# A decode kernel's units in another order behind the second change of layer, and one result row from its own memory

## The chip, the cores and the metric

The kernel runs on one NeuronCore of a Trainium2 chip. The metric is the device time of one execution in microseconds, taken as the median of several runs. The core has TensorE (PE in the profile; PEld is its weight load), VectorE (DVE), ScalarE (ACT), GpSimd (POOL) and SyncE (SP). Here SP issues nearly all DMAs, in program order, and 16 DMA engines carry them out.

## The reference

Two layers, each an attention with a KV cache and then a token mixer, on one new token of B = 2 batches with D = 512 channels:

```
x = x + A(layernorm(x));  x = x + Mix(layernorm(x))      # twice, with the same weights and caches
A:   q = x @ wq (32 heads of 128);  8 kv heads, 4 query heads on each
     p = softmax(q . k_cache / sqrt(128)) over 32768 keys;  o = p @ v_cache;  o @ wo
Mix: u = gelu(layernorm(x)^T * w1 + b1)   (512 x 1792);  u @ w2 + b2
```

Each kv head of each batch has 16 MiB of K and 16 MiB of V in float32, and both layers read all of them: 1 GiB in all. The weights wq and wo of one head together are 2 MiB.

## The kernel before

**Units.** The work is cut into 32 units (layer, batch, head), written out as the list `units` (lines 186 to 191). A unit is 8 chunks of K and 8 of V, each 2 MiB (128 partitions by CK = 4096 columns). Step s belongs to chunk s % 8 of unit s // 8, so there are 256 steps, and a tail.

**One step** (the loop at lines 706 to 722), in this order: issue the load of K chunk s (`load_k`, line 256), multiply it with the query (`k_chunk`, the matmuls of line 277), run the work listed under `pre` for that step, issue the load of V chunk s − 10 (`load_v`, line 332: a unit's V follows its K ten steps later), multiply it with the exponentials in S (`v_chunk`, line 390), run the work listed under `post`. The order on every engine is this program order; nothing is rearranged. Below, K170 is the K chunk of step 170 and V170 the V chunk taken up in step 170, chunk 0 of unit 20. In steps 0 to 93 and from 176 on, two steps go together, with loads of 4 MiB.

**Where the loads go.** One big tile `mem` holds cells of 4096 columns. `buffer` (line 112) hands out the cell, or pair of cells, used least recently: six cells in the paired steps, three (RING) in steps 97 to 175. A load into a cell waits on SP until PE has used what lay there before. In steps 170 to 178 that means: K171 takes the cell of K169, K172 that of V169, V172 that of K170, K173 that of K171, K174 that of K172, K175 that of V172, V175 that of K173. K176, a pair, takes cells in which kept V chunks lie that are read in steps 173 and 174. V178 takes those of K174 and V175.

**Kept V.** Behind the three ring cells lies `kept`: 51 of the 64 parts of V of head 7 (the keeper) that layer 0 loads for one batch and layer 1 reads again (`KEPT`, line 25; `stays`, line 328). Unit 20, (1, 1, 7), reads it in steps 170 to 177: chunks 0, 1, 3, 4, 6 and 7 wholly kept, chunk 2 in part, chunk 5 loaded. Unit 15, (1, 0, 7), does the same for batch 0 in steps 130 to 137. Outside the unpaired steps the ring borrows the cells of kept chunks 1, 3 and 4.

**Weights.** Heads 4 to 7 (RESIDENT) have homes of their own for their weights and load them once. Heads 0 to 3 (`passing`) share the cells of kept chunks 0, 6, 7 and again 0, and are loaded twice: once in layer 0 and, as the kept V has lain there in between, again for unit (1, 0, h). `load_weights` (line 97) is issued in `post` of step s0 − 6 of that unit, where s0 is the unit's first step (lines 661 to 663). `make_q` (line 228) computes the unit's query from wq in steps s0 − 4 and s0 − 3, so between other units' chunks; `out_1` and `out_2` (lines 423, 438) add the unit's result through wo to the batch's row at step s0 + 18.

**Mixer.** When a batch's last unit of a layer is done, `mix_1`, `mix_2`, `hidden_tile`, `hidden_out` and `mix_4` run in the following steps; for (layer 1, batch 0), whose last unit is number 28, `mix_4` (line 628) stands at step 251. It takes S[1] (`row_tile`, line 197), one of the two tiles of exponentials, as memory for the result row, and ACT issues the DMA to `out` from there. The next transpose of scores into S[1] (`turn_scores`, line 308) is that of unit 30 in the same step. Batch 1 ends with unit 31 in `last_mixer`.

Of the kernel before, what the change touches and what calls it, by code (L numbers as in the profile page):

```python
# [36 lines left out]
def gqa_mixer_kernel(ctx: ExitStack, tc: tile.TileContext, x, kt, v, wqo, cols, out):  # L37
# [16 lines left out]
    nc = tc.nc  # L54
    B, D = out.shape
# [30 lines left out]
    kept_columns = sum(KEPT.values()) * QT * DH  # L86
    heads = list(range(HKV))
    passing = [h for h in heads if h not in RESIDENT]
# [3 lines left out]
    kept = mem[:, KEPT0 : KEPT0 + kept_columns]  # L92
# [30 lines left out]
    b2c = cols_sb[:, 3 * FT : 3 * FT + 1]  # L123
# [59 lines left out]
    ends = [h for h in RESIDENT[1:]]  # L183
    keeper = HKV - 1
    assert RESIDENT[0] == keeper and len(ends) == BRIDGE and LAYERS == 2 and B == 2
    units = [(0, b, h) for h in passing for b in range(B)]
    units += [(0, 0, h) for h in ends + [keeper]]
    units += [(0, 1, h) for h in ends] + [(1, 0, keeper), (0, 1, keeper)] + [(1, 0, h) for h in ends]
    units += [(1, 1, keeper), (1, 1, ends[0])]
    units += [(1, b, h) for h in passing for b in range(B)]  # L190
    units += [(1, 1, h) for h in ends[1:]]
    assert sorted(units) == sorted((a, b, h) for a in range(LAYERS) for b in range(B) for h in heads)
    lay = {(a, b): [u for u in units if u[:2] == (a, b)] for a in range(LAYERS) for b in range(B)}

# [2 lines left out]
    def row_tile():  # L197

        return S[HALVES - 1]
# [17 lines left out]
    def unit_of(n):  # L217

        return units[n]
# [230 lines left out]
    ysb, px = {}, {}  # L450
# [177 lines left out]
    def mix_4(key):  # L628

        layer, b = key  # L630
        p = px[key]
        nc.tensor.matmul(p, sel1, ysb[key], start=False, stop=True, skip_group_check=True)
        ysb[key] = row_tile()
        if layer == LAYERS - 1:
            nc.vector.tensor_scalar_add(ysb[key], p, b2c)
            nc.scalar.dma_start(out[b : b + 1, :], ysb[key][:1, :])
        else:
            nc.vector.tensor_copy(ysb[key], p)
            st = work.tile([P, 6], F32, name="ln_st")
            mv = work.tile([P, 2], F32, name="ln_mv")  # L640
            rs = work.tile([P, 1], F32, name="ln_rs")
            nc.vector.bn_stats(st, p)
            nc.vector.bn_aggr(mv, st)
            nc.vector.tensor_scalar_add(rs, mv[:, 1:2], EPS)
            nc.gpsimd.tensor_tensor(rs, rs, half_neg, op=ALU.pow)
            stats[key] = mv, rs
# [7 lines left out]
    for n in range(NU):  # L654
        layer, b, h = unit_of(n)
# [23 lines left out]
        if units[n] == lay[layer, b][-1]:  # L679
            key = (layer, b)  # L680
            at(pre, e - 1, mix_1, key)
            at(post, e, take_rows, key)
            at(pre, e + 1, mix_2, key)
            for f in range(FT + 1):
                k, v_side = divmod(f + 1, 2)

                if f:
                    at(post if v_side else pre, e + 1 + k, hidden_out, key, f - 1, rank=0)
                if f < FT:
                    at(post if v_side else pre, e + 1 + k, hidden_tile, key, f, rank=2)  # L690
            at(post, e + 8, take_rows, key)
            at(pre, e + 9, mix_4, key)
            if layer + 1 < LAYERS:
                at(pre, e + 9, to_columns, key)
# [76 lines left out]
```

## Time and profile before

| what | value |
|---|---|
| median of 3 runs | 2538.9 us (2536.26 to 2538.92) |
| the profiled execution's own time | 2542.73 us |
| its span, first to last instruction | 2541.0 us |
| mean granted TensorE clock | 0.797 |
| busy: PE, PEld, DVE, ACT, POOL | 64%, 17%, 8%, 8%, 0% |
| read from HBM | 1072.20 MB, 422 GB/s over the span |

The profile is of one execution. Busy shares say how long an engine had an instruction running; the DMA share of a stretch is the mean over the 16 DMA engines. A bracket behind an instruction gives how long its engine stood idle before it and what released it; "<-DMA mem<-in_kt_dram" is a K load. Rows of SPq in a timeline are the moments at which SP issued a DMA; an "x3" merges three issues in a row. A row of a timeline with x16 is one 2 MiB chunk on PE, with x32 a pair.

### The profile page before, as it was taken

The page shows a single profiled execution, that of the slowest core. Times are in us where ns is not written, and L with a number is a line of the kernel's source. Part 1 is how long each engine was busy: PE and PEld are TensorE (multiplying, and loading weights), DVE is VectorE, ACT ScalarE, POOL GpSimd, SP SyncE. Part 2 cuts the span into 40 slices and gives each one's busy share as a digit, 9 for nine tenths or more (in the row PEclk, how much of TensorE's full clock was granted, in tenths as well). Part 3 has the DMA queues.
Part 4 walks back from the last instruction along what each step waited for, and adds up shares of the span by engine and source line. Part 5 has one row for each costly group of instructions (what it writes and reads, how often), then busy time and mean ns, then how long its engine had stood idle before and what let it go on. Part 6 is the DMA issues. An engine that isn't in the chain of part 4 may idle for free.

```text
span 2541.0 us, 21411 instructions
## 1 busy us (share of the span) xinstructions
PE 1619.8 (64%) x9700; PEld 426.5 (17%) x9700; DVE 193.5 (8%) x494; ACT 194.6 (8%) x577; POOL 4.9 (0%) x17
## 2 busy tenths in 40 slices
PE   5565656666565666776576765666665666666666
PEld 1111111111111111211121111111111111111112
DVE  1000000000000000110000110010000000000102
ACT  0000000000000000120000110010000000000112
POOL 0000000000000000000000000000000000000000
PEclk8777787777777788888888898787778777778877
DMA  9999999999999999999999999899999999999996
GB/s 413 435 430 429 432 431 431 431 430 433 431 431 430 431 427 428 416 428 421 427 416 426 428 427 427 338 426 429 432 433 430 431 431 430 432 431 430 430 425 283
DMA packets 50068, 1073.58 MB, mean 423 GB/s; under 512 B 5813, under 2 KB 5817, under 8 KB 6458
## 3 DMA queue, kind: packets, MB, share of 16 engines
q1 hardware_dynamic: 49688, 1072.19, 98.7%
q8 instruction: 76, 1.25, 0.2%
q14 instruction: 14, 0.11, 0.0%
q10 hardware_dynamic: 290, 0.03, 0.0%
HBM read 1072.20 MB, written 0.00 MB: 422 GB/s over the span
## 4 chain that ended last, share of the span: by engine, by line
DMA 76%; PE 22%; DVE 1%; issue 0%; ACT 0%; SPq 0%
DMA mem<-in_v_dram 40%; DMA mem<-in_kt_dram 36%; PE scores L277 10%; PE acc L390 10%; PE misc L235 2%; PE misc L247 0%; PE rows L609 0%; DVE hid L244 0%; PE misc L428 0%; PE rows L573 0%; PE misc L419 0%; ACT S L314 0%; ACT hid L620 0%; ACT mem L583 0%; ACT mem L594 0%
## 5 line engine op out<-in xcount | busy, mean ns | idle before, releaser
L390 PE MATMUL acc<-mem,S 128*16 128x512 f32 x4092 | 692.7, 824 | 426.0 <-DMA mem<-in_v_dram 421.1
L277 PE MATMUL scores<-mem,qpad 128*32 128x512 f32 x4096 | 638.1, 767 | 404.0 <-DMA mem<-in_kt_dram 393.3
L314 ACT ACTIVATE S<-S,neg 128x128 f32<-128x128 f32 x256 | 130.5, 513 | 2140.9 <-DVE neg L305 1735.3
L390 PEld LDWEIGHTS acc<-mem,S 128*16 128x16 f32 x4092 | 137.3, 120 | 914.9 <-issue 537.9
L277 PEld LDWEIGHTS scores<-mem,qpad 128*32 128x32 f32 x4096 | 152.7, 132 | 817.3 <-issue 604.3
L235 PE MATMUL misc<-mem,xnT 128*1 128x512 f32 x256 | 118.9, 602 | 1.6 <-issue 1.6
L287 DVE TENSOR_REDUCE mx<-scores 128x1 f32<-128x512 f32 x64 | 44.2, 691 | 464.6 <-PE scores L277 451.1
L428 PE MATMUL misc<-selg,S 128*128 128x4 f32 x248 | 35.3, 266 | 31.1 <-DVE S L425 31.1
L609 PE MATMUL rows<-hid,cols_sb 128*1 128x512 f32 x84 | 49.0, 668 | 8.6 <-ACT hid L620 8.6
L421 DVE RECIPROCAL rl<-misc 128x4 f32<-128x4 f32 x32 | 5.8, 183 | 617.0 <-PE misc L419 617.0
L247 PE MATMUL misc<-one,hid 1*128 1x1 f32 x256 | 33.5, 248 | 29.8 <-DVE hid L244 29.8
L309 DVE STREAM_TRANSPOSE S<-scores 128x512 f32<-128x512 f32 x64 | 44.8, 701 | 90.0 <-PE acc L390 84.3
L314 ACT ACTIVATION_READ_ACCUMULATOR S<-S,neg 128x1 f32 x256 | 47.8, 187 | 0.0
L297 DVE TENSOR_REDUCE m<-misc 1x4 f32<-1x128 f32 x32 | 8.9, 279 | 504.4 <-PE misc L295 504.4
L428 PEld LDWEIGHTS misc<-selg,S 128*128 128x128 f32 x248 | 33.2, 208 | 61.0 <-issue 60.0
L620 ACT ACTIVATE hid<-bcast,bias,scale 128x512 f32<-128x512 f32 x42 | 32.7, 778 | 127.5 <-PE rows L609 111.2
L247 PEld LDWEIGHTS misc<-one,hid 1*128 1x128 f32 x256 | 30.8, 186 | 59.5 <-DVE hid L244 59.5
L441 PE MATMUL rows<-mem,oT 128*1 128x512 f32 x248 | 37.8, 637 | 0.0
L235 PEld LDWEIGHTS misc<-mem,xnT 128*1 128x1 f32 x256 | 19.1, 84 | 70.5 <-issue 69.8
L425 DVE COPY S<-acc 128x512 f32<-128x512 f32 x31 | 21.2, 684 | 84.8 <-PE acc L390 84.8
L244 DVE COPY hid<-misc 1x512 f32<-1x512 f32 x32 | 21.4, 668 | 74.6 <-PE misc L235 71.4
L305 DVE TENSOR_SCALAR neg<-misc 128x4 f32<-128x4 f32 x32 | 5.2, 161 | 245.5 <-PE misc L303 245.5
(109 smaller groups left out, 201.7 us busy)
## 6 DMA issues: line engine op xcount, KB each, us to landing
mem<-in_kt_dram SPq DMA_DIRECT2D x87, 4096.0 KB, 23.7
mem<-in_v_dram SPq DMA_DIRECT2D x85, 4096.0 KB, 24.0
mem<-in_kt_dram SPq DMA_DIRECT2D x82, 2048.0 KB, 12.7
mem<-in_v_dram SPq DMA_DIRECT2D x69, 2048.0 KB, 12.6
mem<-in_wqo_dram SPq DMA_DIRECT2D x12, 2048.0 KB, 28.1
mem<-in_v_dram SPq DMA_DIRECT2D x4, 1280.0 KB, 20.9
mem<-in_v_dram SPq DMA_DIRECT2D x2, 768.0 KB, 22.9
mem<-in_v_dram SPq DMA_DIRECT2D x1, 1024.0 KB, 23.5
```

The source lines that it names most:

```text
L235: nc.tensor.matmul(q_ps[n][:1, :], xnT[layer, b][:, d : d + 1], wq_sb[h][:, d, :], start=(d == 0), stop=(d == DT - 1),)
L244: nc.vector.tensor_copy(q_row[n][:1, :], q_ps[n][:1, :])
L247: nc.tensor.matmul(pt[:, r : r + 1], q_row[n][:1, r * DH : (r + 1) * DH], one[:1, :], start=True, stop=True)
L277: nc.tensor.matmul(sc_ps[n, half][32 * g : 32 * g + 32, :], q, kc[:, (k * NG + g) * w : (k * NG + g + 1) * w], start=(i == 0 and k == 0), ...
L287: nc.vector.tensor_reduce(mx[n][:, half : half + 1], sc_ps[n, half], axis=AX.X, op=ALU.max)
L309: nc.vector.transpose(S[half], sc_ps[n, half])
L314: nc.scalar.activation(s[:, :, h], s[:, :, h], AF.Exp, bias=neg[n][:, h : h + 1], scale=SCALE, accum_out=lsum[n][:, half, h : h + 1],)
L390: nc.tensor.matmul(acc[32 * g : 32 * g + R * QT, :], S[half][:, col : col + R * QT], (own if q < stay else vc)[:, q * w : (q + 1) * w], st ...
L428: nc.tensor.matmul(po[:, :R], asb[:, t * DH : (t + 1) * DH], selg[:, t * R : (t + 1) * R], start=(t == 0), stop=(t == QT - 1),)
L441: nc.tensor.matmul(rows[b][32 * r : 32 * r + 1, :], oT[n][:, r : r + 1], wo_sb[h][:, r, :], start=(units[n] == lay[layer, b][0]), stop=(un ...
L609: nc.tensor.matmul(rows[key[1]][32 * g : 32 * g + 1, :], w2c[:, f : f + 1], hid[key, f], start=(f < NG), stop=(f >= FT - NG),)
L620: nc.scalar.activation(hid[key, f], px[key], AF.Gelu_apprx_tanh, bias=shift[key][:, f : f + 1], scale=slope[key][:, f : f + 1],)
```

## The change

The units from number 20 on stand in another order:

| | 20 | 21 | 22 | 23 | 24 | 25 | 26 | 27 | 28 | 29 | 30 | 31 |
|---|---|---|---|---|---|---|---|---|---|---|---|---|
| before | 1,1,7 | 1,1,4 | 1,0,0 | 1,1,0 | 1,0,1 | 1,1,1 | 1,0,2 | 1,1,2 | 1,0,3 | 1,1,3 | 1,1,5 | 1,1,6 |
| after | 1,1,7 | 1,1,4 | 1,1,5 | 1,0,0 | 1,1,0 | 1,0,1 | 1,1,1 | 1,0,2 | 1,0,3 | 1,1,2 | 1,1,3 | 1,1,6 |

With them move the second loads of the weights of heads 0, 1 and 2: from steps 170, 186 and 202 to 178, 194 and 210. Head 3's stays at 218. The sequence of cells is the same, since it doesn't depend on which unit a step belongs to, other than head 7.

In `mix_4`, batch 0's result row is no longer written to S[1] on 128 partitions but to the last 512 columns of `kept` on one partition (part of kept chunk 2, last read in step 172), and leaves from there.

```diff
-    units += [(1, 1, keeper), (1, 1, ends[0])]
-    units += [(1, b, h) for h in passing for b in range(B)]
-    units += [(1, 1, h) for h in ends[1:]]
+    units += [(1, 1, keeper)] + [(1, 1, h) for h in ends[:2]]
+    *most, final = passing
+    units += [(1, b, h) for h in most for b in range(B)]
+    units.insert(-1, (1, 0, final))
+    units += [(1, 1, final), (1, 1, ends[2])]
...
         nc.tensor.matmul(p, sel1, ysb[key], start=False, stop=True, skip_group_check=True)
-        ysb[key] = row_tile()
         if layer == LAYERS - 1:
-            nc.vector.tensor_scalar_add(ysb[key], p, b2c)
-            nc.scalar.dma_start(out[b : b + 1, :], ysb[key][:1, :])
+            y = kept[:1, kept_columns - D :]
+            nc.vector.tensor_scalar_add(y, p[:1, :], b2c[:1, :])
+            nc.scalar.dma_start(out[b : b + 1, :], y)
         else:
+            ysb[key] = row_tile()
             nc.vector.tensor_copy(ysb[key], p)
```

## The prediction, as put on record before the result

> **What bounds the kernel now.** I read the page first: its slices and its chain of work.
>
> ```profile
> PEclk8777787777777788888888898787778777778877
> DMA  9999999999999999999999999899999999999996
> GB/s 413 435 430 429 432 431 431 431 430 433 431 431 430 431 427 428 416 428 421 427 416 426 428 427 427 338 426 429 432 433 430 431 431 430 432 431 430 430 425 283
> ...
> DMA 76%; PE 22%; DVE 1%; issue 0%; ACT 0%; SPq 0%
> ```
>
> The DMA engines are full in every slice but one and the last, at about 430 GB/s, and 76% of the chain is transfers of K and V. A slice is 63.5 us. The odd one is the 26th (1588 to 1652 us): 338 GB/s. So bytes set the time, and only DMA idle time or bytes can be saved; the change leaves the bytes alone. Next, who holds up the queue on SP: the waits of that queue name line 97, the load of a head's weights, once; then the stretch in windows (columns: from:to, length, busy time of PE, PEld, DVE, ACT, POOL, granted clock, DMA share, GB/s).
>
> ```profile
> SPq L97 <- PE acc L390: 19.8, 1, 19.8
> ...
> 1630.00:1640.00 10.00, 7.00 (x34) 1.36 (x34) 0.69 (x1) 0.00 (x0) 0.00 (x0) 0.59 0.35 149
> 1640.00:1650.00 10.00, 6.21 (x32) 2.23 (x31) 0.16 (x1) 0.00 (x0) 0.00 (x0) 0.67 0.39 128
> ...
> 1680.00:1690.00 10.00, 7.39 (x56) 1.50 (x47) 0.85 (x2) 0.00 (x0) 0.00 (x0) 0.85 0.97 388
> ```
>
> The DMA is idle for 6.5 + 6.1 = 12.6 us, and for 0.3 us more at 1680. The timelines of SP and PE show how it comes about (K170 is the K chunk of step 170, V170 the V chunk taken up in it; W0 the weights of head 0).
>
> ```profile
> 1625.02 0.33 SPq L262 DMA_DIRECT2D mem<-in_kt_dram  x1
> 1645.15 0.33 SPq L97 DMA_DIRECT2D mem<-in_wqo_dram  x1
> 1645.53 0.90 SPq L262 DMA_DIRECT2D mem<-in_kt_dram  x2
> ...
> 1626.36 1.92 PE L277 MATMUL scores<-mem,qpad 128*32 128x512 f32 x16 [1.03 <-DMA mem<-in_kt_dram]
> 1631.25 3.10 PE L390 MATMUL acc<-mem,S 128*16 128x512 f32 x16 [2.97 <-DMA mem<-in_v_dram]
> 1636.10 3.64 PE L277 MATMUL scores<-mem,qpad 128*32 128x512 f32 x16 [1.75 <-DMA mem<-in_kt_dram]
> 1641.47 3.62 PE L390 MATMUL acc<-mem,S 128*16 128x512 f32 x16
> 1644.86 1.35 PE L441 MATMUL rows<-mem,oT 128*1 128x512 f32 x8
> ...
> 1657.82 3.64 PE L277 MATMUL scores<-mem,qpad 128*32 128x512 f32 x16 [11.61 <-DMA mem<-in_kt_dram]
> ...
> 1696.21 5.54 PE L277 MATMUL scores<-mem,qpad 128*32 128x512 f32 x32 [7.91 <-DMA mem<-in_kt_dram]
> ```
>
> SP issues K170 at 1625.02, then stands at W0, whose home is the cell of kept V chunk 0. PE reads that chunk in step 170 (the L390 row at 1641.47, over at 1645.09), and W0 leaves at 1645.15. K171 and K172, behind it in program order, wait with it, though their cells were free at 1628.28 (K169, 1626.36 + 1.92) and 1634.35 (V169, 1631.25 + 3.10).
>
> Two prices come from the same rows. A 2 MiB transfer in a full stream takes 4.87 us: V169 and K170 between the PE starts at 1626.36 and 1636.10 are 9.74. From issue to use an idle queue adds 2.93: W0 and K171 need 1657.82 − 1645.15 = 12.67, less 9.74.
>
> The Trainium skill, "DMA: Bandwidth & Descriptors", Anatomy of one DMA, gives about 2.0 us fixed cost, most of it the receipt of the last byte, fitted on another issuing path. By it the one restart below would cost 0.9 us less and the gain be 0.9 us more; the trace's 2.93 is used.
>
> **Part 1: W0 leaves at step 178 instead of 170.** The wait goes: the read of step 170 is eight steps past. W0's 4.87 us of transfer stay and are paid after 178. What is late next? In steps 170 to 175 only K and 1.25 + 2 MiB of V come from memory (the rest of this head's V is kept) through a ring of three cells, so each load waits for PE to finish an earlier chunk. The kernel runs the same stretch once without a weight load, steps 130 to 137, and I take PE's pace from there.
>
> ```profile
> 1272.65 2.93 PE L277 MATMUL scores<-mem,qpad 128*32 128x512 f32 x16 [2.98 <-DMA mem<-in_kt_dram]
> 1281.35 1.89 PE L277 MATMUL scores<-mem,qpad 128*32 128x512 f32 x16
> 1284.78 1.89 PE L277 MATMUL scores<-mem,qpad 128*32 128x512 f32 x16
> 1286.49 1.89 PE L390 MATMUL acc<-mem,S 128*16 128x512 f32 x16
> 1290.51 1.92 PE L277 MATMUL scores<-mem,qpad 128*32 128x512 f32 x16
> 1298.24 1.92 PE L277 MATMUL scores<-mem,qpad 128*32 128x512 f32 x16
> 1299.98 1.90 PE L390 MATMUL acc<-mem,S 128*16 128x512 f32 x16
> ...
> 1280.00:1285.00 5.00, 5.00 (x52) 1.22 (x44) 1.31 (x2) 0.26 (x1) 0.00 (x0) 0.97 0.82 302
> ...
> 1646.00:1648.00 2.00, 0.21 (x4) 0.00 (x0) 0.00 (x0) 0.00 (x0) 0.00 (x0) 1.00 1.04 254
> ```
>
> There the DMA idles 0.9 us at 1280. Here PE reaches step 171 at 1646.21 (end of the L441 row), 10.11 after K170's start; there 1281.35 − 1272.65 = 8.70, so this one restart is later. The clock granted at 1646 is 1.00, as there. Set 1646.21 against 1281.35 (a shift of 364.86), and land each load at the later of the landing before it and its issue + 2.93, plus its bytes:
> - K171, issued 1628.3: 1636.10 + 4.87 = 1640.97. K172, issued 1634.4: 1645.84. V172 (1.25 MiB, 3.04 us), issued when K170 is used up, 1639.74: 1648.88.
> - K173 needs K171 used: 1646.21 + 1.89 = 1648.10. It starts counting at 1651.03, so the DMA idles 2.15; it lands at 1655.90.
> - K174 after K172 (1286.67 + 364.86 = 1651.53): lands 1660.77. K175 after V172 (1288.38 + 364.86 = 1653.24): 1665.64. V175 after K173 (at 1655.90 + 1.92 = 1657.82, 0.5 behind the pattern): 1670.51.
> - K176 (4 MiB) needs the kept chunk of step 174 read: 1301.88 + 364.86 + 0.5 = 1667.27; + 2.93 is before 1670.51, so no idle; it lands at 1680.25.
>
> Before, K176 landed at 1696.21: 15.96 us earlier, less 4.87 for W0 coming later, is 11.1 us. By shares it is 12.6 + 0.3 − 2.15 = 10.7. I take **10.9 us**; the ends are 12.9 (no idle at all) and the rivals below.
>
> **Part 2: the other moved loads.** W1 goes from step 186 to 194, W2 from 202 to 210, W3 stays at 218. Their homes were last read in steps 176 and 177, so no read is near; W3's home is W0's, whose last reader moves from step 202 to 210. Behind each stand K and V loads on SP, but in that part the queue is deep:
>
> ```profile
> mem<-in_wqo_dram SPq DMA_DIRECT2D x12, 2048.0 KB, 28.1
> ...
> 1800.00:1860.00 60.00, 35.29 (x204) 8.90 (x200) 2.75 (x7) 0.00 (x0) 0.00 (x0) 0.78 1.00 431
> 2220.00:2280.00 60.00, 37.34 (x230) 10.18 (x226) 4.98 (x12) 4.00 (x15) 0.00 (x0) 0.78 1.00 430
> ```
>
> A weight load takes 28.1 us from issue to landing, 23 of them behind earlier loads, and the shares stay at 1.00 (first and last of eight such rows with 1.00 or 1.01). At 9.74 us a step that is a lead of SP of under three steps, so of the eight between 210 and 218 five are left for W3. The bytes cost the same wherever they stand: 0. W0 at 178 stands behind K176, K178 and V178 and ahead of K180, whose step first needs it. The unit now in place 22 has resident weights, so its query waits for no transfer. The last unit and the place of batch 0's last unit (28) don't change, so the mixers and the tail stay.
>
> **Part 3: batch 0's result leaves from its own memory.** DVE now skips a wait; its addition runs on one partition and as many columns, so it costs the same.
>
> ```profile
> 2444.80 0.75 DVE L635 TENSOR_SCALAR S<-bcast,cols_sb 128x512 f32<-128x512 f32 x1 [1.22 <-PE bcast L632]
> 2451.16 0.72 DVE L309 STREAM_TRANSPOSE S<-scores 128x512 f32<-128x512 f32 x1 [5.61 <-DMA out_dram<-S]
> 2451.94 6.56 PE L277 MATMUL scores<-mem,qpad 128*32 128x512 f32 x32 [7.17 <-DVE S L309]
> 2458.57 40.31 SPq L347 DMA_DIRECT2D mem<-in_v_dram  x10
> 2455.00:2460.00 5.00, 5.00 (x36) 1.13 (x32) 0.16 (x1) 0.39 (x2) 0.00 (x0) 0.71 0.90 357
> 2460.00:2465.00 5.00, 4.00 (x42) 1.19 (x38) 0.78 (x2) 0.00 (x0) 0.00 (x0) 1.00 0.95 406
> 2463.24 3.64 PE L277 MATMUL scores<-mem,qpad 128*32 128x512 f32 x32 [0.99 <-DMA mem<-in_kt_dram]
> 2473.05 6.22 PE L390 MATMUL acc<-mem,S 128*16 128x512 f32 x32 [6.18 <-DMA mem<-in_v_dram]
> ```
>
> The transpose into S waits 5.61 us for the result's transfer, PE waits 7.17 us for it, and the next V load leaves late (2458.57). Most of that is covered by queued transfers: the shares lose 0.5 + 0.25 = 0.75 us, and the next two landings are 9.81 apart where 9.74 is a full stream, a loss of 0.07. Between these ends I take **0.5 us**; the new target is read by nothing after step 172.
>
> **Sum.** 10.9 + 0.5 = 11.4 us. Every transfer after it comes earlier by that, and the end behind the last V stays as it is. The profiled execution took 2542.73 us (span 2541.0 and 1.7 around it): 2531.3 in it. That execution is 3.8 above the median 2538.9 (2536.26 to 2538.92), so the forecast for the median is 2538.9 − 11.4 = **2527.5**.
>
> **Rivals.**
> - PE is the bound of steps 171 to 175, at the mean pace of a chunk:
>
> ```profile
> L390 PE MATMUL acc<-mem,S 128*16 128x512 f32 x4092 | 692.7, 824 | 426.0 <-DMA mem<-in_v_dram 421.1
> L277 PE MATMUL scores<-mem,qpad 128*32 128x512 f32 x4096 | 638.1, 767 | 404.0 <-DMA mem<-in_kt_dram 393.3
> ```
>
> Over 256 chunks that is 2.71 us for V and 2.49 for K instead of 1.90. From step 171 to the kept chunk of 174 there are four of each: 3.2 + 2.4 = 5.6 us more. Between them lies the next query's work, 1290.51 − 1288.38 = 2.1 and 1298.24 − 1292.43 − 1.90 = 3.9, together 6.0, which stretches by about 0.3 of itself, 1.8. The kept chunk of 174 is read at 1667.27 + 7.4 = 1674.7, K176 lands at 1674.7 + 2.93 + 9.74 = 1687.4, and the gain is 8.8 − 4.87 + 0.5 = 4.4: 2534.5. For it: the page's clock is 7 or 8 tenths. Against: that is a mean over bursts with pauses, and a dense PE got 0.97 in the twin stretch.
> - Slower: PE stays at half clock through steps 171 to 174. Eight chunks at 3.64 instead of 1.90 are 13.9 us more, the query's work up to 6.0 more: the kept chunk of 174 is read at 1687.2, K176 lands at 1699.8, 3.6 late, W0 comes on top with 4.87, less 0.5: 8.0 slower, 2546.9. It decides once that read ends after 1679 (1696.21 + 0.5 − 4.87 − 12.67). For it: PE was at half clock from 1636 to 1645 though busy throughout (3.64 and 3.62 a chunk). Against: the row of 1646 to 1648.
> - By the Trainium skill, "TensorE: Matmul & The Clock Gate", Part 1, a busy window of about 3.4 us releases the clock, which would rule the half-clock case out; those rows of 3.64 and 3.62, 9 us of work, speak against so firm a rule, so the case keeps a chance.
> - The change doesn't do what it says: SP meets the same wait at a later load, for instance W3 behind its predecessor's last reader. The gap comes back elsewhere and part 3 alone is left: 2538.4. Against: five steps of room.
> - The cells suffice and no idle is left: 12.9 + 0.75 = 13.65, 2525.2.
>
> **How the numbers follow.** Forecast, a gain of 8 to 12.5 us: 0.64. No idle left: 0.10. PE's mean pace, 3 to 8 us: 0.14. The wait comes back: 0.05. Slower: 0.07. The low end is 2525.2 less the 2.7 by which the runs shown differ, 2522.5; the high end 2534.5 lies at the mean-pace case and leaves out half of it, the return of the wait and the slower case: 0.07 + 0.05 + 0.07 = 0.19. About 0.2% (5.1 us) is what a measurement of this kernel can tell from no change; the mean-pace case straddles it, 0.06 above and 0.08 within. Faster 0.64 + 0.10 + 0.06 = 0.80, same 0.08 + 0.05 = 0.13, slower 0.07.
>
> **What would show it.** SP's waits name line 97 no more, and K171 is issued right after K170, near 1628. One dip of 2 to 3 us remains near 1649, then K176 is used near 1680. W0 leaves near 1673 with full shares. DVE's wait for the output's transfer is gone, and the shares from 2450 to 2470 are 1.00. It is wrong if the clock from 1646 to 1667 is 0.5, if another dip stands ahead of K176, or if line 97 waits anew.

## The result, and the profile after

The changed kernel takes 2530.73 us in the median (9 runs, 2529.02 to 2532.41), the kernel before 2538.9 (9 runs, 2536.26 to 2542.07). The ratio is 0.9969 with a 95% interval of 0.9958 to 0.9979: 8.2 us faster in the medians, 5 to 11 by the interval. The forecast was 2527.5, a gain of 11.4. The profiled execution of the changed kernel took 2530.73 us, its own median; that of before, 2542.73, lies 3.8 above its median. So the two profiles differ by 12.0 us and the medians by 8.2, and the question for the experiments is where the 3.8 belong.

The page of the changed kernel: the slice with 338 GB/s is gone.

```profile
DMA  9999999999999999999999999999999999999996
GB/s 415 431 431 431 431 432 431 431 431 431 431 431 431 431 427 426 419 427 423 428 407 428 428 427 428 427 414 432 432 431 431 429 433 431 430 432 431 430 430 282
DMA 77%; PE 21%; DVE 1%; ACT 0%; issue 0%; SPq 0%; ACTq 0%
```

What is left of it is a dip to 414, and beside it the old one at the twin stretch (407). SP's queue in the changed kernel (time of issue, duration; an x3 is three issues merged, and line 262 is now 264, line 347 is 349):

```profile
1625.50 9.67 SPq L264 DMA_DIRECT2D mem<-in_kt_dram  x3
1640.35 0.33 SPq L349 DMA_DIRECT2D mem<-in_v_dram  x1
1645.74 6.30 SPq L264 DMA_DIRECT2D mem<-in_kt_dram  x3
1656.68 0.33 SPq L349 DMA_DIRECT2D mem<-in_v_dram  x1
1667.83 2.04 SPq L264 DMA_DIRECT2D mem<-in_kt_dram  x2
1671.33 0.33 SPq L349 DMA_DIRECT2D mem<-in_v_dram  x1
1671.70 0.44 SPq L97 DMA_DIRECT2D mem<-in_wqo_dram  x1
```

K170, K171 and K172 leave within 10 us, where before K171 and K172 stood for 20 us behind W0. W0 leaves at 1671.70 right behind V178. PE and the windows over the same stretch (line 277 is now 279, line 390 is 392):

```profile
1636.95 3.33 PE L279 MATMUL scores<-mem,qpad 128*32 128x512 f32 x16 [2.15 <-DMA mem<-in_kt_dram]
1641.20 1.91 PE L392 MATMUL acc<-mem,S 128*16 128x512 f32 x16
1643.79 1.90 PE L279 MATMUL scores<-mem,qpad 128*32 128x512 f32 x16
...
1680.20 5.61 PE L279 MATMUL scores<-mem,qpad 128*32 128x512 f32 x32 [8.94 <-DMA mem<-in_kt_dram]
```

```profile
1640.00:1650.00 10.00, 10.00 (x94) 3.37 (x94) 1.64 (x4) 2.19 (x8) 0.00 (x0) 1.00 0.98 398
1650.00:1660.00 10.00, 9.11 (x52) 1.96 (x44) 0.18 (x1) 0.00 (x0) 0.00 (x0) 1.00 1.01 433
1660.00:1670.00 10.00, 8.58 (x65) 2.91 (x68) 1.89 (x4) 0.00 (x0) 0.00 (x0) 0.83 0.91 362
```

K176 is used at 1680.20; worked out was 1680.25. PE is busy 8.6 to 10 us in 10 here, and the DMA share falls to 0.91 in the last row: PE holds the loads up a little, as in the twin stretch (0.82 from 1280 to 1285 before). The wait of DVE at the end is gone too:

```profile
2433.55 0.69 DVE L311 STREAM_TRANSPOSE S<-scores 128x512 f32<-128x512 f32 x1
2434.30 3.64 PE L279 MATMUL scores<-mem,qpad 128*32 128x512 f32 x32 [1.45 <-DVE S L311]
2452.22 5.31 PE L279 MATMUL scores<-mem,qpad 128*32 128x512 f32 x32 [4.37 <-DMA mem<-in_kt_dram]
2462.02 5.32 PE L392 MATMUL acc<-mem,S 128*16 128x512 f32 x32 [4.49 <-DMA mem<-in_v_dram]
```

PE gets K252 1.45 us after its last work and not 7.17. But the next two landings are 9.80 apart, as they were before (9.81).

### The profile page after: what moved, and what is told of

Its sections match the earlier page's. It is cut to its first block, busy times and chain, and to the rows that moved or that the text cites. A ratio compares the mean times of both kernels' runs of the same rounds, so it can differ in the third digit from the quotient of the medians.

```text
span 2529.0 us, 21413 instructions
## 1 busy us (share of the span) xinstructions
PE 1607.9 (64%) x9700; PEld 421.2 (17%) x9700; DVE 193.5 (8%) x494; ACT 194.6 (8%) x577; POOL 4.9 (0%) x17
## 4 chain that ended last, share of the span: by engine, by line
DMA 77%; PE 21%; DVE 1%; ACT 0%; issue 0%; SPq 0%; ACTq 0%
DMA mem<-in_v_dram 42%; DMA mem<-in_kt_dram 35%; PE acc L392 9%; PE scores L279 9%; PE misc L237 2%; PE misc L249 0%; PE rows L611 0%; DVE hid L246 0%; ACT mem L596 0%; PE misc L421 0%; PE misc L430 0%; ACT S L316 0%; PE rows L443 0%; ACT hid L622 0%; ACT mem L585 0%
## 5 line engine op out<-in xcount | busy, mean ns | idle before, releaser
L392 PE MATMUL acc<-mem,S 128*16 128x512 f32 x4092 | 684.2, 815 | 428.4 <-DMA mem<-in_v_dram 424.0
```

Of the source, the lines that this page charges most:

```text
L392: nc.tensor.matmul(acc[32 * g : 32 * g + R * QT, :], S[half][:, col : col + R * QT], (own if q < stay else vc)[:, q * w : (q + 1) * w], st ...
```

## The experiments

**Theory A.** What the change removes is SP's wait for W0 with K171 and K172 behind it. The gap ends when PE has read kept chunk 0 in step 170, so its length follows PE's pace in that step, and that was at its slowest in the profiled execution. The rivals: **B**, the wait is worth 10.9 us always and the new memory of the result row gives 3 back; **C**, the order of the units does something else; **D**, the executions differ elsewhere.

### The order alone, and the result row alone

The first takes the old lines of `mix_4` back into the changed kernel, the second puts only the new ones into the kernel before:

```diff
-            y = kept[:1, kept_columns - D :]
-            nc.vector.tensor_scalar_add(y, p[:1, :], b2c[:1, :])
-            nc.scalar.dma_start(out[b : b + 1, :], y)
+            ysb[key] = row_tile()
+            nc.vector.tensor_scalar_add(ysb[key], p, b2c)
+            nc.scalar.dma_start(out[b : b + 1, :], ysb[key][:1, :])
```

> The new order of units alone; batch 0's result row again leaves from S[1]. Theory A (SP's wait for W0 is what the change removes, and its length follows PE's pace in step 170, which was slow in the profiled execution of before): about 7.7 us faster than before in the median, so 0.5 short of the whole change; the wait of line 97 is gone, DVE's 5.6 us wait for the output's transfer is there. Theory B (the wait is worth the forecast 10.9 us in every execution, and the new memory of the result row gives some 3 us back): 10.9 us faster, more than the whole change.

> The old order of units; batch 0's result row leaves from its own memory. Theory A: 0.1 to 0.75 us faster than before, 0.5 forecast, too little to tell from no change; DVE's wait for the output's transfer is gone and the shares at the end of the stretch around 2450 to 2465 us are full. Theory B: about 3 us slower.

Measured, order alone: 2530.43 us (before on the same chip 2539.25), ratio 0.9963, interval 0.9951 to 0.9975. The result row alone: 2539.99, ratio 0.9999, interval 0.9990 to 1.0007. The order brings all of it, 8.8 us here; the row brings nothing that can be measured, and by its interval it costs 1.8 us at most, so the 3 us of B fall. The row's own profile fits that (PE, result row alone): PE waits 1.46 us and not 7.17, and the landings keep their distance, 9.81 us.

```profile
2443.07 3.64 PE L277 MATMUL scores<-mem,qpad 128*32 128x512 f32 x32 [1.46 <-DVE S L309]
...
2460.33 5.34 PE L277 MATMUL scores<-mem,qpad 128*32 128x512 f32 x32 [4.07 <-DMA mem<-in_kt_dram]
2470.14 5.99 PE L390 MATMUL acc<-mem,S 128*16 128x512 f32 x32 [4.47 <-DMA mem<-in_v_dram]
```

The profile of the order alone is the closest test of part 1, since its step 170 ran at half clock as in the profile of before (PE: K170, V170, K171):

```profile
1635.14 3.64 PE L279 MATMUL scores<-mem,qpad 128*32 128x512 f32 x16 [1.81 <-DMA mem<-in_kt_dram]
1640.51 3.62 PE L392 MATMUL acc<-mem,S 128*16 128x512 f32 x16
1645.06 1.89 PE L279 MATMUL scores<-mem,qpad 128*32 128x512 f32 x16
```

From K170 to K171 it is 9.92 us (10.11 in the prediction). The DMA share from 1640 to 1650 is 0.78, so 2.2 us of idle time, where the prediction had a dip of 2.15, and it is 1.02 and 1.04 in the next two windows of 10 us.

### Only W0 moved, two steps

The kernel before, old order and old row, with one load placed later:

```diff
-            at(post, s0 - 6, load_weights, h)
+            if units[n] == (1, 0, 0):
+                at(post, s0 - 4, load_weights, h, rank=0)
+            else:
+                at(post, s0 - 6, load_weights, h)
```

> The old order of units and the old result row; only W0's load stands two steps later in the program, behind the loads K171, K172 and V172 and just ahead of the unit's query in step 172. Theory A: the order of the units itself is worth nothing, only what stands behind W0 on SP is. W0 is then issued near 1645, when PE has read the kept chunk, but K171 and K172 have gone ahead and no later load is due before 1648; its 4.87 us fill the hole of 2.15 us that the new order leaves there. So 2 us faster than the new order alone, about 9.7 us faster than before, though PE waits some 2 us for W0 in step 172. Theory C (the order of the units does something else for the time, such as spreading the units of batch 1): no more than a few us of gain here.

Measured: 2532.6 us, ratio 0.9973 (0.9962 to 0.9984). With the units in their old order, moving one load by two steps brings 6.7 us. So it is what stands behind W0 on SP that counts, and C falls for the larger part. The extra 2 us did not come. Two rows of this kernel show where they went (PE's wait for W0 ahead of the query; then the window ahead of K176, which PE now releases late):

```profile
1653.23 3.48 PE L235 MATMUL misc<-mem,xnT 128*1 128x512 f32 x4 [2.69 <-DMA mem<-in_wqo_dram]
```

```profile
1670.00:1675.00 5.00, 4.69 (x44) 1.00 (x36) 0.85 (x2) 0.00 (x0) 0.00 (x0) 0.99 0.74 246
```

The hole ahead of K173 was filled, and another of 1.3 us opened ahead of K176. The six runs of this kernel (2532.02 to 2533.98) and the five of the order alone (2529.18 to 2532.13) barely overlap, so it is probably some 2 us slower, and not 2 faster. In the two traces that difference is not in this stretch: by the table below, from K170 to the end of the stream it is 875.1 us here and 874.9 in the order alone, and 1.5 us lie in the tail.

### The wait put back into the changed kernel

```diff
-            at(post, s0 - 6, load_weights, h)
+            at(post, s0 - (14 if units[n] == (1, 0, 0) else 6), load_weights, h)
```

> The changed kernel, both parts, but W0's load is issued in step 170 as before, 14 steps ahead of its unit instead of 6. Theory A: SP waits at line 97 for some 15 to 20 us again, the DMA stands idle for 8 to 12 us near 1640, and the time is that of before less part 3's 0.5 us. Theory C: the gain of the new order stays, 7 to 8 us faster than before.

Measured: 2540.92 us, ratio 1.0004 (0.9995 to 1.0012): the gain is gone, by one load alone. C falls here too; the interval leaves it 1.3 us at most. Its profiled execution took only 2536.10 us, 4.8 below its median, and shows the gap at its shortest (SP's wait, then PE, SP and the windows):

```profile
SPq L97 <- PE acc L392: 15.6, 1, 15.6
```

```profile
1634.65 1.92 PE L279 MATMUL scores<-mem,qpad 128*32 128x512 f32 x16 [1.30 <-DMA mem<-in_kt_dram]
1636.51 1.06 PE L430 MATMUL misc<-selg,S 128*128 128x4 f32 x8
1637.49 1.91 PE L392 MATMUL acc<-mem,S 128*16 128x512 f32 x16
```

```profile
1639.46 0.33 SPq L97 DMA_DIRECT2D mem<-in_wqo_dram  x1
```

```profile
1630.00:1640.00 10.00, 8.70 (x64) 2.34 (x56) 0.85 (x2) 0.00 (x0) 0.00 (x0) 0.83 0.22 93
1640.00:1650.00 10.00, 0.26 (x4) 0.00 (x0) 0.00 (x0) 0.00 (x0) 0.00 (x0) 0.68 0.95 372
```

K170 took 1.92 us here and 3.64 in the profile of before; from K170's start to W0 it is 1639.46 − 1634.65 = 4.81 us, not 9.05, and the idle DMA time 7.8 + 0.5 = 8.3 us, not 12.6.

### The kernel before, profiled three times more

> The kernel before, unchanged, profiled again. Theory A (the length of the gap is set by PE's pace in step 170, which differs from one execution to the next): the time from K170's start to W0's issue lies between 4.8 us (full clock) and 9.1 us (half clock), and the execution's time goes with it, from some 2537 to 2542 us. Theory D (the executions differ elsewhere, in the tail or in the stretch from 130 on, and the gap is the same in all): 9 us in each, whatever the time.

> As before_1: a third profiled execution of the kernel before. Theory A: time and the distance from K170 to W0 go together. Theory D: the distance is 9 us again.

> As before_1: a fourth profiled execution of the kernel before. Theory A: time and the distance from K170 to W0 go together. Theory D: the distance is 9 us again.

Measured: 2540.65, 2542.41 and 2543.41 us. The rows of the first and the third (PE, then SP):

```profile
1634.59 3.50 PE L277 MATMUL scores<-mem,qpad 128*32 128x512 f32 x16 [2.94 <-DMA mem<-in_kt_dram]
1638.02 1.05 PE L428 MATMUL misc<-selg,S 128*128 128x4 f32 x8
1639.01 1.91 PE L390 MATMUL acc<-mem,S 128*16 128x512 f32 x16
```

```profile
1640.98 0.33 SPq L97 DMA_DIRECT2D mem<-in_wqo_dram  x1
```

```profile
1634.62 3.64 PE L277 MATMUL scores<-mem,qpad 128*32 128x512 f32 x16 [1.76 <-DMA mem<-in_kt_dram]
1638.19 1.87 PE L428 MATMUL misc<-selg,S 128*128 128x4 f32 x8
1639.99 3.62 PE L390 MATMUL acc<-mem,S 128*16 128x512 f32 x16
```

```profile
1643.67 0.33 SPq L97 DMA_DIRECT2D mem<-in_wqo_dram  x1
```

The same rows of all traced executions give this table (us; the third column is the start of K170, each one behind it a difference of two starts in the traces; "end of stream" is the start of the last 16 matmuls on V, line 404 or 406; the tail runs from there to SP's issue of the result):

| execution | time | start of K170 | K170 to W0 | K170 to K176 | less K170 to W0 | K176 to end of stream | tail |
|---|---|---|---|---|---|---|---|
| before (as shown) | 2542.73 | 1636.10 | 9.05 | 60.11 | 51.06 | 825.95 | 16.13 |
| before, again | 2540.65 | 1634.59 | 6.39 | 57.29 | 50.90 | 826.11 | 18.21 |
| before, again | 2542.41 | 1635.19 | 8.08 | 59.21 | 51.13 | 826.14 | 17.41 |
| before, again | 2543.41 | 1634.62 | 9.05 | 60.04 | 50.99 | 826.09 | 18.20 |
| result row alone | 2541.65 | 1634.45 | 8.08 | 59.32 | 51.24 | 825.97 | 17.42 |
| wait put back | 2536.10 | 1634.65 | 4.81 | 56.00 | 51.19 | 824.94 | 16.06 |
| matmuls behind the read (below) | 2541.27 | 1634.35 | 9.05 | 60.44 | 51.39 | 825.89 | 16.14 |
| matmuls ahead of the read (below) | 2553.68 | 1634.84 | 20.71 | 72.73 | 52.02 | 825.52 | 16.14 |
| W0 two steps later | 2532.02 | 1635.01 | – | 48.74 | – | 826.37 | 17.42 |
| W0 into the hole (below) | 2531.11 | 1635.03 | – | 49.07 | – | 826.47 | 16.06 |
| order alone | 2530.43 | 1635.14 | – | 45.00 | – | 829.86 | 15.94 |
| changed kernel | 2530.73 | 1636.95 | – | 43.25 | – | 830.89 | 15.19 |

From W0's issue to K176 it is 51 to 52 us in every execution with the wait, and from K176 to the end of the stream 825 to 826 (826.5 at most where W0 came early). What varies is the start of K170, 1634.35 to 1636.95, PE's pace from K170 to W0, 4.81 to 9.05 us without added matmuls, and the tail, 15.2 to 18.2. The three add up one for one: the time less all three is 881.4 to 881.7 us in the first five rows and with the matmuls behind, 880.6 with the wait put back, 882.0 with the matmuls ahead. So A holds for the gap and D for the rest. The time alone doesn't follow the gap: 2543.41, above the 2542 that was expected at most, has the gap of the execution shown, an earlier start and a tail longer by 2.1. In the changed kernel and the order alone the column from K176 on holds W0's 4.87 us as well.

### More work on PE, ahead of the read and behind it

The kernel before with 16 more matmuls in step 170 (`pre`, and for the other kernel `post` with rank 2), whose results nobody uses:

```diff
+    def filler():
+        pt = pmisc.tile([P, 512], F32, name="misc")
+        for k in range(16):
+            nc.tensor.matmul(pt, ident, wq_sb[keeper][:, k % DT, :], start=(k == 0), stop=(k == 15))
+
+    at(pre, 170, filler, rank=0)
```

> The kernel before with 16 more matmuls of 512 columns on PE in step 170, between K170 and the read of kept chunk 0, whose results nobody uses (3.8 us at full clock, 7.3 at half). Theory A (the gap ends when PE has read the kept chunk, so PE's pace up to that read sets the time one for one): W0 leaves 3.8 to 7.3 us later after K170 and the time is 2543 to 2546 us. Rival (PE is off the critical path there, the gap is a matter of the queue alone): no change.

> The kernel before with the same 16 matmuls in step 170, but behind the read of kept chunk 0. Theory A: W0 has left by then, and PE would wait some 11 us for K171 anyway, so no change, near 2539 us. Rival (more work on PE in this stretch costs wherever it stands): as much slower as with the matmuls ahead of the read.

Measured: ahead 2552.29 us, ratio 1.0050 (1.0033 to 1.0067), 12.3 us slower than the 2540.03 of before on that chip; behind 2539.94, ratio 1.0000 (0.9990 to 1.0009). PE and SP's wait, ahead:

```profile
1638.41 14.45 PE L699 MATMUL misc<-mem,ident 128*128 128x512 f32 x32
1652.70 0.95 PE L428 MATMUL misc<-selg,S 128*128 128x4 f32 x8
1653.58 1.91 PE L390 MATMUL acc<-mem,S 128*16 128x512 f32 x16
```

```profile
SPq L97 <- PE acc L390: 32.9, 1, 32.9
```

and behind:

```profile
1644.40 14.00 PE L699 MATMUL misc<-mem,ident 128*128 128x512 f32 x32
1658.34 1.92 PE L277 MATMUL scores<-mem,qpad 128*32 128x512 f32 x16
```

```profile
SPq L97 <- PE acc L390: 19.8, 1, 19.8
```

The matmuls were mis-sized, 14 us and not 3.8 to 7.3, and the time moved with the real size: from K170 to W0 it is 20.71 us and not 9.05, SP's wait grew from 19.8 to 32.9 us, the time by 12.3. The same 14 us behind the read cost nothing that can be measured. PE would have waited there for K171 until 1656 anyway (W0 at 1643.40 and the 12.67 us of the prediction), and that it came to K171 2 us late is not seen in K176, 51.39 us behind W0. A is shown by that: it is PE's path to the read, and not PE's work in this stretch.

### W0 into the hole

The changed kernel with W0 in step 172:

```diff
-            at(post, s0 - 6, load_weights, h)
+            at(post, s0 - (12 if units[n] == (1, 0, 0) else 6), load_weights, h)
```

> The changed kernel with W0's load in step 172 instead of 178, behind K171, K172 and V172, eight steps ahead of its query. Theory A: SP waits for PE's read of kept chunk 0 for some 3 us while no other load is due, W0's bytes fill the DMA's hole ahead of K173, and nothing on PE waits for W0: 1 to 2.5 us faster than the changed kernel, near 2529. Rival: the hole only moves on to K176, whose cells PE frees late, and the time stays at 2530.7.

Measured: 2531.08 us, ratio 0.9965 (0.9951 to 0.9978), not to be told from the 0.9969 of the changed kernel. Its row of K173 on PE and its windows:

```profile
1657.95 3.64 PE L279 MATMUL scores<-mem,qpad 128*32 128x512 f32 x16 [5.07 <-DMA mem<-in_kt_dram]
```

```profile
1665.00:1670.00 5.00, 3.58 (x30) 1.57 (x32) 1.44 (x3) 0.00 (x0) 0.00 (x0) 1.00 0.88 377
1670.00:1675.00 5.00, 5.00 (x52) 1.21 (x44) 0.85 (x2) 0.00 (x0) 0.00 (x0) 1.00 0.64 213
```

W0's bytes go ahead of K173, so PE waits 5.07 us for that and frees the cells of K176 later: SP issues K176 at 1671.88 and not at 1667.83 as in the changed kernel, and 0.6 + 1.8 = 2.4 us of idle DMA stand ahead of it. The hole moved on, as the rival said.

## Why the prediction was right, and where its size was off

- **The bound and the wait** were right: removing that one wait brings the gain (8.8 us by the order alone, 6.7 by one load moved two steps, none left with the wait put back), and nothing was changed in the bytes.
- **Part 1, the mechanism:** right. K176 was worked out for 1680.25 and came at 1680.20, but so close by luck: K170 started 0.85 later, and from K170 to K176 it was 43.25 us, worked out as 44.15. In the order alone, whose step 170 ran as slowly as in the profile of before, it was 45.00, and the dip of 2.15 came as worked out. In the changed kernel the remaining idle time came ahead of K176 instead (0.9 us in 1660 to 1670): PE ran step 170 faster and step 174, whose read frees the cells of K176, slower (2.41 and 3.18 us for K174 and V174; 1.92 and 1.90 for their twins at 1298.24 and 1299.98).
- **Part 1, the size: this is the step that was off.** The 12.6 us of idle DMA were one execution's, with PE at half clock all through step 170: 9.05 us from K170 to W0. Other executions show 8.08, 6.39 and 4.81. I set the forecast against the median, 3.8 us below that execution, and took the full gap off all the same. Against its own execution the term holds: from K170 to the end of the stream the two profiles shown differ by 60.11 + 825.95 − 43.25 − 830.89 = 11.9 us, and the order alone differs from that of before by 11.2. Against the medians the gain is 8.2, at the low end of the 8 to 12.5 that were forecast, and its interval reaches below.
- **How far that explains the size:** in the executions that were only timed the gap isn't seen, so that it is shorter there is inferred. An estimate from the table: with 881.5 us for the rest, and a start of K170 and a tail anywhere in the ranges of the seven executions that have the wait and no matmuls ahead of the read, the median of 2538.9 leaves 3 to 7 us for the gap, 2 to 6 less than 9.05. That covers the 3.2 us by which the forecast was off. But these seven have gaps of 7.8 us in the mean and took 2541.2 us in the mean, more than the medians. And 0.9 to 1.8 of the 3.8 us probably lie ahead of step 170: the execution shown started K170 at 1636.10, the other six at 1634.35 to 1635.19.
- **Part 2:** right, the later moved loads cost nothing: K176 to the end of the stream is 825 to 826.5 us in all, plus W0's 4.87 where it comes after.
- **Part 3, 0.5 us:** nothing that can be seen. The interval of the row alone is wider than 0.5 us, but from K176 to the end of the stream, the stretch with that place in it, its profile has 825.97 us and that of before 825.95. The low end, the distance of the landings, was the one to take.
- **The rivals:** PE's mean pace did not come, PE was at 1.00 from 1640 to 1660. The half-clock case neither, though what spoke for it stands: the last repeated profile of before ran step 170 at half clock (3.64 and 3.62 us a chunk, granted clock 0.50 from 1634 to 1644). The rule of the Trainium skill's "TensorE: Matmul & The Clock Gate", Part 1, is full clock after about 3.4 us of sustained work. At this place the traces don't show it; 1.87 us between the two chunks are matmuls of 4 columns, and no run here says whether these count as work. The return of the wait did not come: none of SP's waits in the changed kernel is at line 97.

What stays open: the tail was 15.2 to 16.1 us in the table's four executions with the new order and 16.1 to 18.2 in its eight with the old one. PE's clock in it differs (0.69, 0.84 and 0.50 in the three windows of 5 us from 2520 in the first repeat of before; 1.00, 1.00 and 0.66 from 2510 in the changed kernel). Its code is the same, and whether that is chance was not tried.

## What to carry to other kernels

In a queue that issues in order, a load is not early when it stands early: it is early when what lies in its target has been read. Put a load whose target is freed late behind the loads that are already free to go, even if it is then needed soon. And where the engine that frees the target changes its pace from one execution to the next, take the price of the wait from several executions, or scale it, before setting it against a median.

## What the runs showed of the hardware that I had not expected

- The same instructions at the same place ran at different granted clocks: K170 took 1.92 us at 1.00 (1634 to 1640, wait put back), 3.64 at 0.50 (1636 to 1644, the profile of before), and 2.85, 2.90 and 3.50 in others, in executions of kernels that don't differ up to there. A load waited for PE at this place, and so PE's pace went into the time of a kernel bound by DMA. Nine runs of before spread over 5.8 us, nine of the changed kernel over 3.4.
- A float32 matmul of 512 columns that writes 128 rows took 14.45 / 16 = 0.90 us (granted clock 1.00 from 1640 to 1650) and 14.00 / 16 = 0.88 behind the read; the 8 of a K chunk, which write 32 rows each in four groups, 1.90 us together, 0.24 each. Taking one for the other made the filler four times as long as meant.
